# Later pairs' loads behind the first broadcast, and a fourth buffer for exponentials, in a planned attention and gated-MLP kernel

## Chip, cores and metric

The kernel runs on one core of one Trainium2 chip. The metric is device time in microseconds (us) of one execution; lower is better.

## What is computed

Eight batches, eight heads each, 576 positions, head dimension 64, all in float32. Per head, causal attention with a decay bias: the running sum `cum` of max(s, 0) along the sequence gives a bias -(cum_i - cum_j) for every query and key, cut at 0. The heads' outputs of one batch, side by side, are the 512 wide input of a gated MLP with a three-tap convolution along the sequence.

```python
def _attn_ref(q, k, v, s):
    scores = scale * np.matmul(q, k.transpose(0, 1, 3, 2))
    cum = np.cumsum(np.maximum(s, 0.0), axis=-1)
    bias = -(cum[:, :, :, None] - cum[:, :, None, :])
    scores = np.where(causal, -1000000000.0, scores + np.minimum(bias, 0.0))
    scores = scores - np.max(scores, axis=-1, keepdims=True)
    attn = np.exp(scores)
    attn = attn / (np.sum(attn, axis=-1, keepdims=True) + 1e-09)
    return np.matmul(attn, v)

def _moe_ref(x, w_in, conv_w, w_out):
    h = np.maximum(x @ w_in, 0.0)          # 512 -> 1024
    conv_out = ...                         # three taps along the sequence, per channel
    gate = 1.0 / (1.0 + np.exp(-conv_out))
    return (h * gate @ w_out)              # 1024 -> 512
```

## The kernel before

**Pairs.** Work is cut into 32 pairs of heads, four to a batch; `pair(p)` makes the tasks of one. A pair's queries and keys come in one load (`qk`, tile `raw`, line 1015). ACT or DVE rounds them to a high part (`hi`, line 1027), POOL or DVE takes the low rest (`lo`, line 1031), both in tile `s`. A shifted score is then formed to find each row's maximum: matmuls `sh` (line 1097), with a mask added by matmuls on line 1104 for the first seven pairs, and on DVE 12 reductions `mx` (line 1129) per pair that add the broadcast prefix sums `bb` (line 1059, a transfer that copies two rows of `cum_d` to all partitions) and keep the maximum in `r`. A transpose `turn` (line 1155), ACT `rt` (line 1163) and a DMA `ds` into `eq` (line 1171) bring the maxima into a row. Then come the 48 score matmuls `sc` (line 1208), 12 exponentials on ACT into `pt` (line 1223), five causal cuts `mk` on POOL (line 1241), the sums over keys `sum` (line 1323) and the product with the values `pv` (line 1266).

**The normalising chain.** After `sum`, ACT copies the sums (`gd`, guard, line 1339), a DMA regroups them (`rc`, line 1345), DVE takes the reciprocal (line 1350), a DMA writes it to DRAM (`ri`, line 1355), a DMA pair spreads it over the partitions (`rb`, line 1365), and DVE multiplies `pv` by it (`nm`, norm, line 1373); ACT and DVE or POOL then split the result into `x` (lines 1388, 1392). There is one set of buffers for `rs`, `rc` and `ri` together, taken by `gd` and given back when `rb` has landed, and one for `pv` in PSUM, given back by the norm.

**Gated MLP.** For each batch and half of the sequence, `h` (line 1423) are the matmuls with `w_in`, 12 to a block of 128 channels, and `o` (line 1512) those with `w_out`. `h` of a batch needs the four pairs of that batch and the weights, which are loaded (line 880), put together from 64 bit words and split into two parts on ACT, DVE and POOL during the first pairs.

**What sets the order.** Every piece of work is a task with a cost in us, the tasks that it needs and the buffers that it takes. `Sched.play` lets the five engines run through these costs, and each engine takes the ready task with the smallest due time; the due times are the table `DUE`, one number for a task, in sixteenths of a us. The order so found is what each engine runs, strictly in a row; a semaphore wait holds all that stands behind it. `opts` of a task names the engines that may do it and the cost on each; a third entry `True` keeps a DVE task and a POOL task that both have it from being planned at the same time. `follow(a, b)` offers `b` only when `a` has been started. Where PE would have nothing to do, the planner puts in a matmul on zeros (tile `still`, line 1559), up to its time 112.

**Buffers.** `BUFS` counts them. The fifth number, `NPT`, is that of `pt`, one for a head; a pair takes two at its first scores and gives them back after `sum` and `pv`. `setup` values share their room: `s_sb` and `ones` lie in `PT_t[1]`, `cum` and `grid` in `PT_t[2]`.

**The start.** `s` is loaded, DVE makes `cum` (lines 763, 764), then `grid` and `ncr` (lines 771 to 777); SP writes `cum` (line 789) and `ncr` (line 791) to DRAM and fetches the first broadcasts (line 1059). `bx` (lines 798, 802) are rows for the scores, stored to `rows_d` (line 815). POOL makes constants (`ident`, lines 716 to 731; `masks`, lines 702 to 709: a memset and four selects; `pads`, lines 737, 739). The first bias transposes on PE (line 830) take the PSUM bank of the first reduction.

Of the kernel before, what the change touches and what calls it, by code (L numbers as in the profile page):

```python
# [27 lines left out]
BUFS = 2, 2, 3, 3, 3, 5, 3, 2  # L28
# [520 lines left out]
def kernel(  # L549
# [192 lines left out]
    def c_ind(t):  # L742
        def run(e):
# [8 lines left out]
            c_pads(i))  # L752
        for i in range(NE)
    ]
    t_ident = add("ident", [("POOL", 4.3)], [], -189.5, c_ident)
    t_ind = [
        add(f"ind{i}", [("ACT", 0.72)], [t_masks], -187 + i, c_ind(EQ_t[i])) for i in range(NEQ)
    ]
# [216 lines left out]
    def link():  # L975
        for n, g in sorted(groups.items()):
# [6 lines left out]
            for (a, _), (c, _) in zip(seq, seq[1:]):  # L983
                sch.follow(a, c)

    direct = []
    last_ek, last_v, last_nm = [None], [None], []


    L = NT - 1  # L990
# [637 lines left out]
```

## Time and profile before

| | us |
|---|---|
| median of 3 runs | 767.01 |
| lowest and highest | 760.92, 767.8 |
| profiled execution | 766.71 |
| its span | 765.0 |
| granted TensorE clock, mean share | 0.989 |
| busy: PE, PEld, DVE, ACT, POOL | 744.2, 669.3, 513.5, 455.6, 363.1 |

The span runs from the first to the last instruction; the profiled execution was 1.7 us longer than its span. PE is the TensorE with its matmuls, PEld its weight loads, DVE VectorE, ACT ScalarE, POOL GpSimd, SP the engine that issues all DMAs here. A busy PE may be busy with matmuls on zeros, and at the lower of two clocks (2.4 and 1.2 GHz; 0.50 in a row is the lower one).

### The profile page before, as it was taken

Reading aid. Unit: us, or ns where it says so; the run is one execution under the profiler, and the core shown is the slowest. Engines: PE = TensorE matmul, PEld = TensorE weight load, DVE = VectorE, ACT = ScalarE, POOL = GpSimd, SP = SyncE. Lnnn points to the kernel's source line nnn. Section 1 sums busy time; section 2 is a strip of 40 time slices with the busy share of each in tenths; the row PEclk is TensorE's granted clock in tenths of the full one; section 3 lists DMA queues with packets and bytes.
Section 4 is the critical chain, followed back from the end, with each engine's and each line's share of the span. In section 5 each row is a group of like instructions: output and inputs, shape, how many; then the busy total and the mean of one; then the engine's idle time right before and its main releaser. Section 6 shows DMA issues by size and latency. Waiting matters only on the chain.

```text
span 765.0 us, 20449 instructions
## 1 busy us (share of the span) xinstructions
PE 744.2 (97%) x7868; PEld 669.3 (87%) x7868; DVE 513.5 (67%) x1404; ACT 455.6 (60%) x1070; POOL 363.1 (47%) x444
## 2 busy tenths in 40 slices
PE   8998999999999999999999999999999999999998
PEld 6675778898988888898988889898888999899998
DVE  7488987566776757677775776777686676633632
ACT  5276777375665656566674756556566646654643
POOL 6053435574566455545554655545435546612212
PEclk9599999999999999999999999999999999999999
DMA  6865852324333241424322342242414221111001
GB/s 192 262 212 185 271 185 66 129 66 128 93 106 111 56 128 65 128 93 122 98 79 87 98 132 79 78 143 80 127 48 122 90 82 43 43 41 40 17 25 39
DMA packets 55160, 80.18 MB, mean 105 GB/s; under 512 B 14042, under 2 KB 34842, under 8 KB 55002
## 3 DMA queue, kind: packets, MB, share of 16 engines
q1 hardware_dynamic: 55061, 78.87, 33.3%
q8 instruction: 61, 1.00, 0.5%
q14 instruction: 38, 0.30, 0.1%
HBM read 67.48 MB, written 10.98 MB: 103 GB/s over the span
## 4 chain that ended last, share of the span: by engine, by line
PE 79%; DVE 8%; issue 5%; DMA 4%; ACT 2%; POOL 1%; SPq 0%; DVEq 0%; POOLq 0%; ACTq 0%
PE ps L1423 25%; PE ps L1512 25%; PE ps L1208 11%; PE pv L1266 10%; PE ps L1097 4%; DVE ps L1129 3%; PE ps L1323 3%; DMA rb<-ri_d 2%; DMA ri_d<-ri 2%; ACT pt L1223 1%; PE ps L1559 1%; DVE r L1129 1%; DMA bb<-cum_d 1%; DVE ct L1454 1%; DVE rb L1373 1%
## 5 line engine op out<-in xcount | busy, mean ns | idle before, releaser
L1512 PE MATMUL ps<-u,wo 128*128 128x288 f32 x1536 | 218.2, 298 | 1.1 <-ACT ob L1529 0.5
L1423 PE MATMUL ps<-x,wi 128*128 128x290 f32 x1536 | 217.6, 298 | 0.3 <-DVE x L1392 0.2
L1423 PEld LDWEIGHTS ps<-x,wi 128*128 128x128 f32 x1536 | 209.2, 190 | 2.2 <-ACT pt L1223 0.5
L1512 PEld LDWEIGHTS ps<-u,wo 128*128 128x128 f32 x1536 | 206.9, 188 | 4.0 <-ACT pt L1223 1.7
L1223 ACT ACTIVATE pt<-ps,bias_sb 128x288 f32<-128x288 f32 (+4 forms) x384 | 152.9, 479 | 64.6 <-PE ps L1208 64.4
L1484 POOL TENSOR_TENSOR u<-ct,u 128x576 fp32r<-128x576 f32 x64 | 92.4, 1446 | 187.8 <-ACT u L1480 144.1
L1454 DVE SCALAR_TENSOR_TENSOR ct<-ps,cw_sb,ct 128x288 f32<-128x288 f32 (+1 forms) x256 | 130.2, 514 | 69.6 <-ACT ct L1441 67.1
L1129 DVE CUSTOM_DVE_ANT_0 ps<-ps,bb 128x64 f32<-128x64 f32 (+4 forms) x320 | 134.3, 451 | 47.3 <-PE ps L1097 23.1
L1208 PE MATMUL ps<-s 64*128 64x288 f32 (+4 forms) x1152 | 113.8, 304 | 8.6 <-DVE r L1129 7.5
L1208 PEld LDWEIGHTS ps<-s 64*128 64x128 f32 x1152 | 91.0, 187 | 17.3 <-DVE r L1129 12.4
L1241 POOL TENSOR_SCALAR_AFFINE_SELECT pt<-pt 128x256 f32<-128x256 f32 (+1 forms) x160 | 69.9, 450 | 74.6 <-ACT pt L1223 56.4
L1070 POOL TENSOR_SCALAR_AFFINE_SELECT bb<-bb 128x256 f32<-128x256 f32 (+1 forms) x125 | 52.6, 429 | 98.4 <-DVE r L1129 81.9
L1266 PE MATMUL pv<-pt,v 128*32 128x448 f32 (+4 forms) x1536 | 94.6, 389 | 3.3 <-DVE rb L1373 3.3
L1436 ACT ACTIVATE ps<-ps 128x289 f32<-128x289 f32 x128 | 50.8, 397 | 72.8 <-PE ps L1423 67.1
L1031 POOL TENSOR_TENSOR s<-raw,s 128x1152 fp32r<-128x1152 f32 x31 | 88.8, 2865 | 6.2 <-ACT s L1027 3.9
L1266 PEld LDWEIGHTS pv<-pt,v 128*32 128x32 f32 x1536 | 59.2, 110 | 34.6 <-issue 24.6
L1466 ACT ACTIVATE ct<-ct 128x288 f32<-128x288 f32 x128 | 56.2, 440 | 38.6 <-DVE ct L1454 38.0
L1472 DVE TENSOR_TENSOR ct<-ct,ps 128x288 f32<-128x288 f32 x128 | 57.1, 449 | 21.7 <-ACT ct L1466 20.9
L1441 ACT ACTIVATE ct<-ps,cw_sb 128x288 f32<-128x288 f32 x128 | 63.8, 500 | 5.0
L1097 PE MATMUL ps<-s 64*128 64x288 f32 (+4 forms) x384 | 60.3, 348 | 1.3 <-DVE ct L1472 1.1
L1208 PE MATMUL ps<-eq,ek 64*128 64x288 f32 (+4 forms) x384 | 59.7, 301 | 0.0
L1129 DVE DVE_READ_ACCUMULATOR2_ANT r<- 128x1 f32 x384 | 54.1, 141 | 0.0
(89 smaller groups left out, 700.6 us busy)
## 6 DMA issues: line engine op xcount, KB each, us to landing
raw<-qk SPq DMA_DIRECT2D x32, 576.0 KB
bb<-cum_d SPq DMA_DIRECT2D x32, 576.0 KB
v<-vp SPq DMA_DIRECT2D x32, 320.0 KB
rb<-ri_d SPq DMA_DIRECT2D x64, 144.0 KB
outT<-ob SPq DMA_DIRECT2D x64, 144.0 KB
w<-w_in SPq DMA_DIRECT2D x8, 512.0 KB
w<-w_out SPq DMA_DIRECT2D x8, 512.0 KB
rows_d<-bx SPq DMA_DIRECT2D x1, 1215.0 KB
```

The costliest lines, as they stand in the source:

```text
L1031: tt_on(e)(st[:, 0:2, :], R_t[raw.slot], st[:, 2:4, :].bitcast(F32), op=ALU.subtract)
L1097: nc.tensor.matmul(dst[j], l, S_t[sb.slot][r, 2, c0:c1], start=True, stop=not (early and diagonal(tau, c1)),)
L1129: nc.vector.tensor_tensor_reduce(out=src, in0=src, in1=in1, scale=1.0, scalar=acc if c0 else -3.0e38, op0=ALU.add, op1=ALU.max, accum_out=acc,
L1208: nc.tensor.matmul(dst[j], l, m, start=(k == 0), stop=(k == 3))
L1223: nc.scalar.activation(PT_t[pts[j].slot][0:jt, O_T[t] + c0 : O_T[t] + c1], bank(pb, o, o + c1 - c0)[0:jt], AF.Sigmoid, bias=bias_sb[0:jt, ...
L1241: nc.gpsimd.affine_select(out=reg, in_=reg, pattern=[[0, 2], [1, min(P, W_T[t])]], compare_op=ALU.is_ge, fill=0.0, base=0, channel_multipl ...
L1266: nc.tensor.matmul(pvt[gs, o0 : o0 + c1 - c0], vt[0:jt, t, gs], PT_t[pts[g // 2].slot][0:jt, O_T[t] + c0 : O_T[t] + c1], start=(t == 0), s ...
L1423: nc.tensor.matmul(bank(hb, 0, XW), l, r, start=(k == 0), stop=(k == len(seq) - 1))
L1441: nc.scalar.activation(C_t[ct.slot][:, i, :], bank(hb, 2 * hf, 2 * hf + HS), AF.Copy, scale=cw_sb[:, 3 * f + 1 : 3 * f + 2],)
L1454: nc.vector.scalar_tensor_tensor(cc[:, lo:hi], bank(hb, hf + sh + lo, hf + sh + hi), cw_sb[:, 3 * f + k : 3 * f + k + 1], cc[:, lo:hi], op ...
L1484: tt_on(e)(uu[:, 1], C_t[ct.slot], uu[:, 0].bitcast(F32), op=ALU.subtract)
L1512: nc.tensor.matmul(bank(pb, 0, HS), l, r, start=(fp == 0 and k == 0), stop=(fp == NF // 2 - 1 and k == len(seq) - 1),)
```

## The change

- `NPT`, the number of buffers for heads' exponentials, goes from 3 to 4 (one more 64x64 memset at the start).
- Loads of `raw` for pairs 2 and up are offered only after the first broadcast `bb0` has been started.
- In the planner, `bb0` counts 400,000 bytes more, and nine costs of setup tasks are changed; `cum`, `grid` (and `rest` as before) are kept apart in time from POOL tasks that have the same mark.
- The table `DUE` is a new one, of the same length. So the order is new on every engine.

```diff
-BUFS = 2, 2, 3, 3, 3, 5, 3, 2
+BUFS = 2, 2, 3, 3, 4, 5, 3, 2
...
-    -4437, -31564, -3194, -3762, -3297, -3396, -3426, -2970, -2895, -2949, -3684, -32749, -26067,
...
+    9452, 6483, 13492,
...
-    t_masks = add("masks", [("POOL", 3.6)], [], -190, c_masks)
+    t_masks = add("masks", [("POOL", 4.4)], [], -190, c_masks)
...
-    t_ident = add("ident", [("POOL", 4.3)], [], -189.5, c_ident)
+    t_ident = add("ident", [("POOL", 2.9)], [], -189.5, c_ident)
...
-    t_ones = add("ones", [("DVE", 0.4)], [], -298, lambda e: nc.vector.memset(ones, 1.0))
+    t_ones = add("ones", [("DVE", 0.55)], [], -298, lambda e: nc.vector.memset(ones, 1.0))
...
-    t_cum8 = add("cum", [("DVE", 2.0)], [t_s, t_ones], -170, cum_chain)
+    t_cum8 = add("cum", [("DVE", 2.0, True)], [t_s, t_ones], -170, cum_chain)
...
-    t_cum = add("grid", [("DVE", 2.4)], [t_cum8], -169, grid_chain)
+    t_cum = add("grid", [("DVE", 1.5, True)], [t_cum8], -169, grid_chain)
...
-    t_rest = add("rest", [("DVE", 1.6, True)], [t_cum], -140, rest)
+    t_rest = add("rest", [("DVE", 0.8, True)], [t_cum], -140, rest)
...
-    t_bmm = add("bias_mm", [("PE", 1.2)], [t_rest, t_ident], -140, bias_mm, alloc=[b_ps])
+    t_bmm = add("bias_mm", [("PE", 0.6)], [t_rest, t_ident], -140, bias_mm, alloc=[b_ps])
...
+    first_bb = []
...
         t_bb = add(f"bb{p}", [("SP", 0.4)], [t_cum_d], a_sh - BBA, load_bb, alloc=[bb],
-                   nbytes=2 * P * S * 4)
+                   nbytes=2 * P * S * 4 + (400_000 if p == 0 else 0))
+        if p == 0:
+            first_bb.append(t_bb)
+        elif p > 1:
+            sch.follow(first_bb[0], t_load)
```

All lines of the changed file lie 1 to 6 further down than in the one before.

The queue of SP at the start, before: `raw0`, `raw1` are the two buffers for queries and keys (pairs 2 and 3 use them anew), `bb0` and `bb1` those for the broadcasts.

```order
L789 DMA cum_d_111<-pt_96 64x576
L791 DMA base_d_112<-ncr_118 64x10
L1059 DMA bb0_91<-cum_d_111 128x2x576
L1015 DMA raw0_81<-qk 128x1152
L1059 DMA bb1_92<-cum_d_111 128x2x576
L787 DMA base_sb_93<-base_d_112 5x32x2 x2
```

The same rows of the change:

```order
L790 DMA cum_d_111<-pt_96 64x576
L792 DMA base_d_112<-ncr_118 64x10
L1061 DMA bb0_91<-cum_d_111 128x2x576
L1017 DMA raw0_81<-qk 128x1152
L1061 DMA bb1_92<-cum_d_111 128x2x576
L788 DMA base_sb_93<-base_d_112 5x32x2 x2
```

Nothing has moved here: the load of the third pair stood behind the first broadcast already.

DVE at the start, before, from the making of `ncr` to the first reduction (`s1` is pair 1, `s0` pair 0):

```order
L774 TENSOR_SCALAR ncr_118<-pt_96 64x9
L777 MEMSET ncr_118 64x1
L822 SCALAR_TENSOR_TENSOR pt_96<-pt_96 64x576
L802 TENSOR_SCALAR bx_119<-pt_96,ncr_118 64x576 x2
L895 SCALAR_TENSOR_TENSOR ct0_107<-ct0_107 128x24
L1031 TENSOR_TENSOR s1_84<-raw1_82,s1_84 128x1152
L1129 ISA ps4_69,r0_99<-ps4_69,bb0_91 128x64
```

DVE at the same place in the change:

```order
L775 TENSOR_SCALAR ncr_118<-pt_96 64x9
L778 MEMSET ncr_118 64x1
L1033 TENSOR_TENSOR s0_83<-raw0_81,s0_83 128x1152
L823 SCALAR_TENSOR_TENSOR pt_96<-pt_96 64x576
L803 TENSOR_SCALAR bx_119<-pt_96,ncr_118 64x576 x3
L1033 TENSOR_TENSOR s1_84<-raw1_82,s1_84 128x1152
L896 SCALAR_TENSOR_TENSOR ct0_107<-ct0_107 128x24
L902 SCALAR_TENSOR_TENSOR ct0_107<-ht_106,ct0_107 128x24
L1135 ISA ps0_65,r0_99<-ps0_65,bb0_91 128x288
```

The low parts of pair 0 have come to DVE, behind `ncr`; a third row set `bx` too; and the first reduction is now that on bank `ps0_65`, which the bias transposes wait for.

POOL at the start, before, after the last memset of `onehot`:

```order
L737 MEMSET ek2_87 128x640
L739 MEMSET ek2_87 10x576 x2
L1031 TENSOR_TENSOR s0_83<-raw0_81,s0_83 128x1152
L737 MEMSET ek1_86 128x640
L739 MEMSET ek1_86 10x576 x2
L702 MEMSET v1_95 128x640
L705 AFFINE_SELECT v1_95<-v1_95 64x640
```

POOL at the same place in the change:

```order
L703 MEMSET v1_95 128x640
L706 AFFINE_SELECT v1_95<-v1_95 64x640
L710 AFFINE_SELECT v1_95<-v1_95 64x640
L706 AFFINE_SELECT v1_95<-v1_95 64x640
L710 AFFINE_SELECT v1_95<-v1_95 64x640
L738 MEMSET ek1_86 128x640
```

The subtraction for pair 0 has left POOL, and the memset and four selects of `masks` have come to the front.

ACT after the exponentials of pair 0, before; L891 and L886 are weights, L1339 is the guard of pair 0, and the exponentials on L1223 behind it are those of pair 1:

```order
L1223 ACTIVATE pt_96<-ps0_65,bias_sb_76 128x320
L891 ACTIVATE w1_5122_356<-w1_10240_354,tail_sb_78 128x512
L886 ACTIVATE w1_5121_355<-w1_10240_354 128x512
L886 ACTIVATE w0_5121_352<-w0_10240_351 128x512
L891 ACTIVATE w0_5122_353<-w0_10240_351,tail_sb_78 128x512
L886 ACTIVATE w2_5121_358<-w2_10240_357 128x512
L891 ACTIVATE w2_5122_359<-w2_10240_357,tail_sb_78 128x512
L1339 ACTIVATE rs_103<-ps1_66 128x144
L938 CAST wi_79<-w1_5122_356 128x4x128
L938 CAST wi_79<-w0_5122_353 128x4x128
L1163 ACTIVATE rt0_101<-ps0_65,base_sb_93 10x64 x2
L1223 ACTIVATE pt_96<-ps1_66,bias_sb_76 128x288
```

ACT at the same place in the change:

```order
L1229 ACTIVATE pt_96<-ps1_66,bias_sb_76 128x320
L887 ACTIVATE w1_5121_361<-w1_10240_360 128x512
L892 ACTIVATE w1_5122_362<-w1_10240_360,tail_sb_78 128x512
L887 ACTIVATE w2_5121_364<-w2_10240_363 128x512
L892 ACTIVATE w2_5122_365<-w2_10240_363,tail_sb_78 128x512
L1229 ACTIVATE pt_96<-ps1_66,bias_sb_76 128x288
L1229 ACTIVATE pt_96<-ps3_68,bias_sb_76 128x288
L1229 ACTIVATE pt_96<-ps4_69,bias_sb_76 128x288
L1229 ACTIVATE pt_96<-ps5_70,bias_sb_76 128x288
L887 ACTIVATE w0_5121_358<-w0_10240_357 128x512
L892 ACTIVATE w0_5122_359<-w0_10240_357,tail_sb_78 128x512
L1345 ACTIVATE rs_103<-ps0_65 128x144
```

With the fourth buffer, four exponentials of pair 1 stand ahead of the guard of pair 0. On PE likewise: 16 of pair 1's 48 score matmuls stand before the sums of pair 0 and the other 32 before its `pv`, where before all 48 stood behind `pv`.

## Rows read from the trace of the kernel before

**Rows 1.** The page: the span, and the granted TensorE clock in 40 equal slices of it, in tenths of full speed.

```profile
span 765.0 us, 20449 instructions
...
PEclk9599999999999999999999999999999999999999
```

**Rows 2.** Busy time of each engine in four stretches (from:to, length, then PE, PEld, DVE, ACT, POOL busy with their instructions, granted clock, DMA share, GB/s).

```profile
0.00:17.60 17.60, 14.76 (x119) 11.55 (x119) 13.11 (x27) 9.95 (x14) 13.27 (x29) 1.00 0.56 174
17.60:34.70 17.10, 17.09 (x88) 10.78 (x90) 9.59 (x46) 2.52 (x8) 0.00 (x0) 0.50 0.95 296
34.70:105.50 70.80, 67.24 (x965) 49.52 (x963) 58.40 (x170) 52.86 (x117) 29.67 (x36) 1.00 0.66 213
105.50:740.00 634.50, 623.23 (x6543) 575.82 (x6540) 423.97 (x1147) 379.37 (x908) 315.85 (x376) 1.00 0.29 89
```

**Rows 3.** The matmuls on zeros (line 1559) in the stretch from 34.7 to 105.5 us, as a group of PE's lines (busy us, mean ns of one), and the group of `pv` there with the idle time before it and who ended it.

```profile
L1559 PE MATMUL ps<-still 64*128 64x256 bf16 (+1 forms) x104 | 14.8, 272 | 0.1
L1266 PE MATMUL pv<-pt,v 128*32 128x448 f32 (+4 forms) x240 | 14.6, 390 | 3.3 <-DVE rb L1373 3.3
```

**Rows 4.** Timeline of the start (start us, length us, engine, line, operation; in brackets the idle time before it and who ended it): DVE, POOL and SP.

```profile
7.07 3.22 DVE L774 TENSOR_SCALAR ncr<-pt 64x9 f32<-64x9 f32 x1
9.65 0.74 DVE L822 SCALAR_TENSOR_TENSOR pt<-pt 64x576 f32<-64x576 f32 x1
10.33 1.71 DVE L802 TENSOR_SCALAR bx<-pt,ncr 64x576 fp32r<-64x576 f32 x2
12.06 1.34 DVE L1031 TENSOR_TENSOR s<-raw,s 128x1152 fp32r<-128x1152 f32 x1
...
3.44 0.63 POOL L737 MEMSET ek<- 128x640 f32 x1
7.06 2.64 POOL L1031 TENSOR_TENSOR s<-raw,s 128x1152 fp32r<-128x1152 f32 x1 [1.55 <-ACT s L1027]
12.69 1.29 POOL L705 TENSOR_SCALAR_AFFINE_SELECT v<-v 64x640 f32<-64x640 f32 x1
14.05 0.71 POOL L709 TENSOR_SCALAR_AFFINE_SELECT v<-v 64x640 f32<-64x640 f32 x1
...
5.79 0.50 SPq L789 DMA_DIRECT2D cum_d<-pt  x1
10.35 0.46 SPq L791 DMA_DIRECT2D base_d<-ncr  x1
```

**Rows 5.** The chain of waits, in order of time (start us, us, what).

```profile
10.86 5.21 DMA bb<-cum_d
...
48.22 3.72 DMA ri_d<-ri
...
52.57 5.11 DMA rb<-ri_d
...
57.77 0.76 DVE rb L1373
...
77.30 3.53 PE ps L1208 x48
...
101.83 0.77 DVE rb L1373
```

**Rows 6.** Stretches of 1 us with the same columns as Rows 2.

```profile
8.00:9.00 1.00, 1.00 (x9) 0.52 (x10) 1.00 (x1) 1.00 (x2) 1.00 (x1) 1.00 0.00 0
...
16.00:17.00 1.00, 0.00 (x0) 0.00 (x0) 0.75 (x5) 0.65 (x2) 0.32 (x1) 1.00 1.01 410
...
18.00:19.00 1.00, 0.99 (x5) 0.49 (x3) 1.00 (x7) 0.33 (x1) 0.00 (x0) 0.50 1.68 438
```

**Rows 7.** Timeline of DVE and PE from the first reduction to the first scores.

```profile
9.59 6.28 PE L1559 MATMUL pv<-still 64*128 64x256 bf16 x56
16.25 0.23 DVE L1129 CUSTOM_DVE_ANT_0 ps<-ps,bb 128x64 f32<-128x64 f32 x1 [2.85 <-DMA bb<-cum_d]
17.59 0.70 PE L830 MATMUL ps<-ident,pt 64*128 64x64 f32 x5 [1.71 <-DVE r L1129]
26.91 4.23 PE L1559 MATMUL ps<-still 64*128 64x256 bf16 x19
28.23 0.40 DVE L1129 CUSTOM_DVE_ANT_0 ps<-ps,bb 128x192 f32<-128x192 f32 x1
32.55 1.09 PE L1208 MATMUL ps<-s 64*128 64x288 f32 x6
```

**Rows 8.** Timeline of pair 0 after its scores: exponentials, weights and guard on ACT, sums on PE, and the first matmuls of the MLP.

```profile
33.91 1.85 ACT L1223 ACTIVATE pt<-ps,bias_sb 128x288 f32<-128x288 f32 x4 [1.82 <-PE ps L1208]
36.11 2.99 ACT L1223 ACTIVATE pt<-ps,bias_sb 64x64 f32<-64x64 f32 x8 [0.35 <-PE ps L1208]
39.63 1.24 ACT L886 ACTIVATE w<-w 128x512 f32<-128x512 f32 x2
41.73 1.77 PE L1323 MATMUL ps<-pt,onehot 128*32 128x144 f32 x54
43.60 0.29 ACT L1339 ACTIVATE rs<-ps 128x144 f32<-128x144 f32 x1 [0.82 <-PE ps L1323]
...
105.48 1.88 PE L1423 MATMUL ps<-x,wi 128*128 128x290 f32 x12
```

**Rows 9.** The group of the `sh` matmuls over the whole span (busy us, mean ns of one).

```profile
L1097 PE MATMUL ps<-s 64*128 64x288 f32 (+4 forms) x384 | 60.3, 348 | 1.3 <-DVE ct L1472 1.1
```

468 rows, old and new, of the table DUE are left out of this document.

## Prediction

> **What bounds the kernel now.** I read the page first, then busy time by stretches, then the chain of waits and the timeline of the first 110 us. The span is 765.0 us, and the profiled execution took 766.71 us, 1.7 us more, close to the median of 767.01 us, so the sum is made against 766.7 [rows 1]. From 105.5 to 740 us PE is busy for 623.23 of 634.50 us at full clock and runs no matmul on zeros: PE bounds this stretch, and its work there is the same in the change [rows 2]. What can be won lies before 105.5 us. There PE seems busy too, but much of it is not work. In the first 17.6 us hardly any work is done. From 17.6 to 34.7 us the granted clock is 0.50, the lower of the two levels [rows 2]. From 34.7 to 105.5 us PE spends 14.8 us on 104 matmuls on zeros and waits 3.3 us, all of it for the norm, while DVE is busy 58.4 of 70.8 us and ACT 52.9 [rows 2, 3].
>
> In that last stretch the normalising chain sets the pace. The norm of pair 0 starts at 57.77 us and that of pair 3 at 101.83: three rounds in 44.06 us, 14.7 us each [rows 5]. Within the first, the reciprocals' store takes 3.72 us and the spread 5.11 [rows 5]. There is one set of buffers for this, so a guard can come only after the last spread has landed, and `pv` of the next pair waits for the norm. The first matmul of the MLP is at 105.48, 3.65 us after the start of norm 3 [rows 5, 8].
>
> **The change, part by part.**
>
> *The loads behind the first broadcast.* In the queue of SP the third pair's load already follows `bb0`, and the rows there are the same in both orders. So the new rule by itself moves nothing and is costed at 0, between -0.5 and +0.5 us for later loads, nearest to the equal rows.
>
> *DVE's start.* The making of `ncr` takes 3.22 us, beside a subtraction on POOL of 2.64 us; the broadcasts' write `base_d` waits for it until 10.35, and `bb0` stands behind that and goes at 10.86 [rows 4, 5]. In the change the subtraction is on DVE, behind `ncr`. A tensor-scalar of ten columns is at most as long as one of `bx`, 0.86 us, so `ncr` ends at 7.2 to 7.9 instead of 10.30, and `base_d` can go 2.4 to 3.1 us sooner. Then `bb0` waits for `cum_d`, issued at 5.79: the DMA engines are idle from 8 to 9 us [rows 4, 6], so I put its landing at 8.5 and the issue of `bb0` there, 2.3 us sooner; with its 5.21 us it lands at 13.7 instead of 16.07 [rows 5]. DVE by then has done, from 7.2 on, two subtractions of 1.34, 0.74, three `bx` of 0.86 and two small ones of about 0.2, some 6.4 us, and is free at 13.6 [rows 4]. The first reduction starts at 13.8, not 16.25 [rows 7].
>
> *PE's wait and the clock.* PE ends its 56 zeros at 15.87, stands still until 17.59 because the bias transposes need a bank that the third reduction gives free, and in the slice from 18 us the clock is 0.50 [rows 6, 7]. In the change the 57 zeros (0.112 us each, after 45 instead of 48 at the start) end at about 15.6, and the bank's reduction is now the first, done at 14.4. The wait of 1.71 us is gone, and I expect the clock to stay at its upper level.
>
> *From the first reduction to the first scores.* 24 reductions of the two pairs take from 16.25 to 28.63 before, 12.4 us with the waits among them [rows 7]. In the change they take 13.8 to 26, less some 1.5 us of waits for a slow PE and plus 1 us for the bias. The second transpose then stands ready at 26, after 19 zeros that took 4.23 us at half clock and take half of that at full. Seven zeros and the scores follow: 27.5 us instead of 32.55 [rows 7]. At half clock this would be 30.
>
> *Pair 0 to its guard.* Before, the exponentials start 1.36 us after the scores and take until 39.1, and the guard starts at 43.60 [rows 7, 8]. In the change ACT begins at 28.9 and needs 4.9 us for 12 exponentials; then four weight passes of 0.62 (2.5 us), four exponentials of pair 1 (1.85), two more passes (1.3): 39.5 [rows 8]. Beside this, POOL's cuts and PE's sums are done by 38. I take the guard at 39.8, with 0.3 for handing over: 3.8 us sooner. The scores came 5 us sooner; the pieces that now stand ahead of the guard take 1.2 us back.
>
> *The rounds.* The chain's buffers are not changed. Four rounds of 14.7 us lead from guard 0 to norm 3, now at 98.0. Per round the same transfers lie between (a broadcast, values, keys, two or three weights), in other places, and SP now has a load of `ek` that waits for the next pair's scores ahead of the store. I take no change, with 0.8 us a round to either side.
>
> *The fourth buffer.* With it, scores may run ahead of `pv`. By the first MLP matmul the order has 296 score matmuls instead of 240, 92 `sh` instead of 84, one more transpose, and as many sums and `pv`. At 3.53 us for 48 and 0.157 for one `sh` this is 4.1 + 1.3 + 0.3 = 5.7 us of work done by then that before came later [rows 5, 9]. The MLP's first matmul stands behind eight of these score and six `sh` matmuls, 0.6 + 0.9 = 1.5 us, so it comes 3.65 + 1.5 after norm 3, at 103.2 instead of 105.5. The gain is 2.3 + 5.7 = 8.0 us. PE has room for that: 27 zeros fewer behind the first scores are worth 3.8 us [rows 3], and the rest comes from the 5 us at the start. The extra memset and PE's allocations lie beside other work.
>
> *The rest.* Behind 105.5 us idle time is 11.3 us of 634.5 [rows 2]. A new table may move this by 3 us either way; I take 0.
>
> Sum: 766.7 - 8.0 = 758.7, say 758.8 us.
>
> **A rule of the skill against it.** In the trace, a select of `masks` takes 1.29 us when it starts beside DVE's subtraction and 0.71 alone, and `ncr` stood still beside POOL's subtraction [rows 4]. In the change the four selects run from about 4.1 us beside the prefix sums. If each can hold up one of DVE's steps for its 0.71 us, `ncr` ends at 10.0, `bb0` goes at 10.5, and all that follows is 2 us later, while PE's wait is still gone or short: 760.8. The Trainium skill, SBUF — State Buffer, section Who interferes with whom, says that VectorE and GpSimd share a pair of ports under an exclusive lock, that whichever starts first holds it for its whole instruction, and that the other "fully blocks"; the trace agrees with its 3.22 us, and by that rule the planner's mark on `cum` and `grid` doesn't protect them, as `masks` has none.
>
> **Rivals.**
> - *The lock:* as above, 760.8. For it: the two rows. Against: memsets on POOL beside the same DVE steps, from 3.44 us on, delayed nothing [rows 4].
> - *The clock falls all the same:* the reductions still pace PE with short waits from 17 to 26 us. Scores at 30 instead of 27.5, guard at 42: 766.7 - 8.0 + 2.5, plus a first score block at half speed, about 762.
> - *The rounds grow by 1.5 us:* the chain is longer by what now stands ahead on ACT and SP. 4 x 1.5 = 6 us back: 765. The same time comes out if the change does not do what it says and only the order is another.
> - *Slower:* the load of `ek` ahead of the reciprocals' store waits for scores which wait for banks that ACT frees only behind the guard. Each round is held by 4 us: 16 - 8 = 8 us, 775. It turns slower than now from 2 us a round.
> - *More:* rounds shorter by 0.8 us and less idle time in the MLP stretch: 754.
>
> **How the numbers follow.** The measurement tells about 1% from no change, 7.7 us, so faster means below 759.3. Chances: the forecast 0.48 (755.5 to 762, six in ten of it below 759.3), more 0.12, the lock 0.12, the clock 0.12, grown rounds 0.10, slower 0.06. Faster: 0.29 + 0.12 + 0.02 + 0.02 = 0.45; slower 0.06; the same 0.49. The range goes from 752 to 768: it leaves out the slower case and a tail of the better one.
>
> **What would show it.** In the changed profile: `ncr` short and `bb0` issued near 8.5 us; no PE wait at 16 us and a clock of 1.00 from 16 to 35; the first scores near 27.5, the guard of pair 0 near 39.8, norms 14.7 us apart, norm 3 near 98, the first MLP matmul near 103; from there the same idle time. Selects of 1.3 us or a late `ncr` would show the lock; waits of SP ahead of the reciprocals' store the grown rounds. Wrong most easily: the length of a round, which counts four times.

## The result, and the profile after

| | before | after |
|---|---|---|
| median of 13 executions, us | 766.40 | 770.76 |
| lowest and highest | 760.57, 769.38 | 767.59, 775.25 |
| profiled execution, its span | 766.71, 765.0 | 773.5, 771.8 |
| mean granted clock of that execution | 0.989 | 0.991 |

The ratio is 1.0079, 95% interval 1.0054 to 1.0103: the change costs 0.8%. I had forecast 758.8 us, a gain of 1%, and a range that ended at 768.

The page of after: span, and granted clock in 40 slices.

```profile
span 771.8 us, 20376 instructions
...
PEclk9989999999999999999999999999999999999999
```

Half of the plan worked: the 5 in [rows 1] is gone. But an 8 stands in the third slice, where before had a 9.

Stretches of after, cut at its own first MLP matmul, 113.24 us (columns as in [rows 2]; the last three rows are stretches of 1 us).

```profile
17.60:34.70 17.10, 16.85 (x163) 12.61 (x163) 11.42 (x54) 5.77 (x17) 3.35 (x4) 1.00 0.92 285
34.70:113.24 78.54, 68.34 (x942) 49.19 (x938) 59.20 (x173) 55.16 (x121) 35.42 (x43) 0.91 0.65 201
113.24:771.80 658.56, 644.35 (x6637) 594.04 (x6637) 414.74 (x1144) 386.54 (x917) 323.06 (x380) 1.00 0.28 85
47.00:48.00 1.00, 0.25 (x4) 0.12 (x2) 0.08 (x1) 0.89 (x2) 0.79 (x3) 1.00 1.00 361
...
49.00:50.00 1.00, 0.00 (x0) 0.00 (x0) 0.97 (x2) 0.95 (x2) 0.00 (x0) 0.50 0.86 250
93.00:94.00 1.00, 1.00 (x7) 0.68 (x5) 0.68 (x2) 1.00 (x4) 1.00 (x1) 0.50 0.73 279
```

The same last stretch of before, from its first MLP matmul to the end:

```profile
105.48:765.00 659.52, 645.08 (x6708) 597.43 (x6702) 432.37 (x1165) 390.32 (x933) 320.15 (x379) 1.00 0.28 86
```

Three things are to be seen. From 17.6 to 34.7 us the clock is at its upper level, as forecast ([rows 2]: 0.50). From 34.7 us to the first MLP matmul the mean clock is 0.91, which makes some 14 of 78.5 us at the lower level (an estimate from the mean), and that stretch is 78.5 us instead of 70.8. From the first MLP matmul on, after needs 658.56 us for 65 weight loads fewer (6,637 for 6,702), where before needs 659.52: the work that was brought forward is missing there, but the time isn't.

What PE waited for from 26 to 114 us in after (us in total, times, longest):

```profile
PE ps L1329 <- DVE r L1135: 4.4, 1, 4.4
PE ps L1103 <- ACT pt L1229: 2.5, 1, 2.5
PE ps L1565 <- ACT rt L1169: 1.9, 1, 1.9
PE ps L1214 <- ACT rs L1345: 1.1, 1, 1.1
```

Before, the only waits of PE there were 3.3 us for the norm [rows 3]. After, 0.2 us is for the norm, and the rest for reductions, exponentials, a bias copy and a guard. The largest is read from the chain of waits of after (start us, us, what):

```profile
45.21 5.10 DMA bb<-cum_d
...
50.44 0.63 DVE ps L1135
...
51.60 3.34 PE ps L1329 x41
54.94 0.56 PE ps L1103 x2
...
57.28 0.62 DVE rb L1379
...
57.94 2.18 PE pv L1272 x25
```

In before the chain to norm 0 runs through the reciprocals' store and the spread [rows 5]. Here it runs through a broadcast of prefix sums, `bb3`, that pair 3's reductions need. It lands at 50.31. The sums of pair 1 stand on PE behind one of these reductions, because they use its bank, so PE stands still; products stand behind the sums, two reductions behind those products, and norm 0 behind those in DVE's row.

Why `bb3` is so late is seen in the timeline of after. SP:

```profile
40.50 1.24 SPq L1351 DMA_DIRECT2D rc<-rs  x2
...
42.71 0.94 SPq L881 DMA_DIRECT2D w<-w_in  x2
44.30 0.34 SPq L1361 DMA_DIRECT2D ri_d<-ri  x1
45.21 0.37 SPq L1061 DMA_DIRECT2D bb<-cum_d  x1
```

PE, and DVE below it:

```profile
41.64 0.33 PE L1103 MATMUL ps<-s 64*128 64x320 f32 x2
...
51.60 3.34 PE L1329 MATMUL ps<-pt,onehot 128*32 128x144 f32 x56 [4.35 <-DVE r L1135]
```

```profile
43.20 0.35 DVE L1135 CUSTOM_DVE_ANT_0 ps<-ps,bb 128x192 f32<-128x192 f32 x1
...
50.44 0.63 DVE L1135 CUSTOM_DVE_ANT_0 ps<-ps,bb 128x448 f32<-128x448 f32 x1 [0.38 <-DMA bb<-cum_d]
```

There are two buffers for broadcasts, so `bb3` needs pair 2's to be used up. Pair 2's last products (41.64) now stand on PE behind the sums of pair 0 and scores of pair 1. That scores of pair 1 stand so early only a fourth buffer for exponentials allows; that the products stand behind them is the new table's choice. And five weight passes of DVE, from 40.32 on, stand ahead of pair 2's four last reductions (43.20 to 45.19); the products were done by then, so the passes end last. Only then can SP send `bb3`.

### The profile page after: what moved, and what is told of

It reads as the page before. It is cut to its first block, busy times and chain, and to the rows that moved or that the text cites. A ratio compares the mean times of both kernels' runs of the same rounds, so it can differ in the third digit from the quotient of the medians.

```text
span 771.8 us, 20376 instructions
## 1 busy us (share of the span) xinstructions
PE 745.4 (97%) x7852; PEld 668.1 (87%) x7852; DVE 500.0 (65%) x1397; ACT 457.6 (59%) x1068; POOL 373.4 (48%) x454
## 4 chain that ended last, share of the span: by engine, by line
PE 81%; DVE 6%; DMA 5%; issue 3%; ACT 3%; POOL 0%; SPq 0%; DVEq 0%; POOLq 0%; ACTq 0%
PE ps L1518 25%; PE ps L1429 24%; PE ps L1214 12%; PE pv L1272 11%; PE ps L1103 4%; PE ps L1329 4%; DMA w<-w_in 2%; DVE ps L1135 2%; DMA bb<-cum_d 2%; DVE ct L1460 1%; ACT pt L1229 1%; DMA ek<-bx 1%; DMA ek<-rows_d 1%; DVE r L1135 1%; PE ps L1161 0%
## 5 line engine op out<-in xcount | busy, mean ns | idle before, releaser
L1429 PE MATMUL ps<-x,wi 128*128 128x290 f32 x1536 | 220.1, 299 | 2.8 <-DVE ct L1478 2.3
L1460 DVE SCALAR_TENSOR_TENSOR ct<-ps,cw_sb,ct 128x287 f32<-128x287 f32 (+1 forms) x256 | 130.0, 514 | 80.2 <-ACT ct L1447 75.1
L1135 DVE CUSTOM_DVE_ANT_0 ps<-ps,bb 128x192 f32<-128x192 f32 (+4 forms) x320 | 133.8, 452 | 58.0 <-PE ps L1103 30.7
L1214 PE MATMUL ps<-s 64*128 64x288 f32 (+4 forms) x1152 | 118.1, 304 | 8.0 <-DVE r L1135 5.8
L1214 PEld LDWEIGHTS ps<-s 64*128 64x128 f32 x1152 | 94.9, 185 | 18.0 <-DVE r L1135 12.2
L1272 PE MATMUL pv<-pt,v 128*32 128x448 f32 (+4 forms) x1536 | 96.4, 395 | 0.2 <-DVE rb L1379 0.2
L1033 POOL TENSOR_TENSOR s<-raw,s 128x1152 fp32r<-128x1152 f32 x30 | 85.0, 2832 | 8.3 <-ACT s L1029 8.3
L1272 PEld LDWEIGHTS pv<-pt,v 128*32 128x32 f32 x1536 | 58.2, 111 | 34.2 <-issue 27.0
L1214 PE MATMUL ps<-eq,ek 64*128 64x288 f32 (+4 forms) x384 | 63.7, 299 | 0.0
L1103 PE MATMUL ps<-s 64*128 64x288 f32 (+4 forms) x384 | 59.2, 345 | 2.6 <-ACT pt L1229 2.5
```

The source lines that it names most:

```text
L1033: tt_on(e)(st[:, 0:2, :], R_t[raw.slot], st[:, 2:4, :].bitcast(F32), op=ALU.subtract)
L1103: nc.tensor.matmul(dst[j], l, S_t[sb.slot][r, 2, c0:c1], start=True, stop=not (early and diagonal(tau, c1)),)
L1135: nc.vector.tensor_tensor_reduce(out=src, in0=src, in1=in1, scale=1.0, scalar=acc if c0 else -3.0e38, op0=ALU.add, op1=ALU.max, accum_out=acc,
L1214: nc.tensor.matmul(dst[j], l, m, start=(k == 0), stop=(k == 3))
L1272: nc.tensor.matmul(pvt[gs, o0 : o0 + c1 - c0], vt[0:jt, t, gs], PT_t[pts[g // 2].slot][0:jt, O_T[t] + c0 : O_T[t] + c1], start=(t == 0), s ...
L1429: nc.tensor.matmul(bank(hb, 0, XW), l, r, start=(k == 0), stop=(k == len(seq) - 1))
```

## The experiments

In all edits `put(names, ahead)` moves tasks in the order found by the planner to directly ahead of another task; `zeros(n, ahead)` adds matmuls on zeros. The clock differs from one execution of the same program to the next, so each median mixes several; where it matters, executions of like clock are compared.

**The load rule.** After, with the third pair's load ahead of `bb0` again:

```diff
+    put("qk2", "bb0")
```

> The changed kernel, with one thing undone: the load of the third pair's queries and keys stands in SP's queue ahead of the first broadcast of prefix sums again, nothing else moves. If the order of these two transfers matters, the first broadcast, issued at 9.13 us in the changed kernel, comes some 0.4 us later and shares the engines with 576 KB more, so it lands 1 to 2 us later, pair 0's reductions follow, and the end is 1 to 1.5 us later: 772. Rival: the second broadcast (issued 10.28, 8.04 us to land) and PE's own work end this stage, so nothing moves: 770.8.

Measured: 772.95 us (767.26 to 778.13), ratio to before 1.0107 (1.0065 to 1.0150); after had 1.0079. `bb0` goes 1.1 us later (10.26), but first scores and first sums come at the same times as in after (28.0, 36.0). The median is higher by executions at a clock of 0.982 and less, which after has none of; at 0.996 and 0.997 three take 767.26 to 770.95 us, and after at 0.996 to 0.998 767.59 to 769.40. The rule that gives the change its name has no effect that can be seen here.

**The start alone.** Before, with only the start of the change, three buffers, and before's order for the rest:

```diff
+    by["lo0"].eng = "DVE"
+    put("ones", "still")
+    put("tail", "pads0")
+    put("lo0", "rest")
+    put("masks", "pads2")
```

> The kernel before (three buffers, its own order) with the new start alone: the subtraction for pair 0's low halves on DVE in place of POOL, DVE's and POOL's start in the order of the change; from the first scores on every engine keeps the order of before. Theory of the prediction: PE no longer waits 1.71 us at 15.9, the clock stays at 1.00 in 17.6 to 34.7, pair 0's guard comes 3 to 4 us earlier and the rounds take 14.7 us as before: 758 to 761. Rival: the next wait (pair 3's broadcast, weights) takes the gain back whatever the order is: 765 to 767.

Measured: 764.16 us (760.89 to 766.28), 0.9984 (0.9956 to 1.0013), between the two expected ranges. PE's wait of 1.71 us [rows 7] is gone, and the clock falls all the same, in stretches of 1 us:

```profile
17.00:18.00 1.00, 0.82 (x5) 0.42 (x5) 1.00 (x6) 0.00 (x0) 0.00 (x0) 1.00 1.02 284
18.00:19.00 1.00, 1.00 (x7) 0.57 (x8) 0.28 (x2) 0.00 (x0) 0.00 (x0) 0.72 1.23 329
19.00:20.00 1.00, 0.89 (x5) 0.37 (x3) 0.57 (x3) 0.00 (x0) 0.00 (x0) 0.50 0.85 203
```

PE is busy for 0.82 to 1.00 of each of these, and the longest wait behind the first zeros is 0.18 us. That it is enough to end the wait of 1.71 us, as I had it, is refuted.

**Zeros for the clock, three times.** In before (e6), in before with the new start (e7), and in after (e2, in front of the three waits):

```diff
# e6, before
+    zeros(14, "bias_mm")
+    zeros(6, "sh1.0")
+    zeros(4, "sh1.1")
# e7, before with the new start
+    zeros(4, "bias_mm")
+    zeros(6, "sh1.0")
+    zeros(4, "sh1.1")
# e2, after
+    zeros(36, "sum1")
+    zeros(20, "nm1")
+    zeros(14, "rt5")
```

> The kernel before, with 24 more zero matmuls on PE between 15.9 and 20 us: 14 ahead of the transposes that wait until 17.59 and 10 ahead of the next products. Nothing else moves. Theory: the kernel before has a clock drop of 17.07 us in this place in its profile, and its executions fall into two groups by the clock of the whole run: 759.7 to 762.0 where it is 1.000, some 767 where it is 0.989. If the empty stretch brings the drop, the zeros hold the clock and nearly all executions are at 760 to 762. Rival: the drop has another cause, and the median stays at 766 or loses up to 1 us to the zeros.

> The new start alone on the kernel before (as in the run start alone, 764.16), with 14 more zero matmuls on PE behind pair 0's first products. Theory of the clock: the start alone still fell to half clock at 18.45 us in its profile though PE no longer waited 1.7 us; its executions at a clock of 1.000 took 760.9 to 762.6. With PE filled as it is in the changed kernel (x22 matmuls in 16 to 18 us against x15) the clock stays at 1.00 and the median is 760 to 762. Theory of the prediction (an earlier start is worth its 3 to 4 us where the order behind it is that of before): 757 to 759. Rival: the drop stays: 764.

> The changed kernel, with 36, 20 and 14 more zero matmuls on PE, at the places of its idle stretches at 47.2, 71.2 and 91.0 us: the waits stay, only the clock is kept. Theory of the clock: no drop at 48.5 and 92.9; the 3.8 and 6.8 us that PE worked at half clock shrink by half, 5.3 us, and the time is 765.5. Theory of the waits: what follows each gap waits for DVE and ACT and not for PE, so a full clock gives back 2 us at most: 769. If the zeros stand in the way, 771 to 773.

Measured: e6 764.82 us, 0.9999 (0.9969 to 1.0029): the mean clock is at least 0.995 in every execution (in 31 of before's 102), so zeros in this place mostly keep it, but in a late start they cost what the clock gives. e7 **762.24 us (759.69 to 764.38), 0.9956 (0.9931 to 0.9982)**: the fastest kernel of this study. Its first scores come at 27.6 us, its first MLP matmul at 101.1, and seven of twelve executions keep a clock of 1.000. These take 759.69 to 762.60 us, and before at 1.000 takes 759.65 to 762.96: what e7 wins over before is the clock, and the earlier start of the prediction (757 to 759 expected) isn't to be seen in the time. But e7 has the change's start, with first scores as late as in after (27.6 and 27.9), ahead of three buffers and before's order, and is at its first MLP matmul 12.2 us sooner than after. So nearly all of the loss, with the falls of the clock at 48 and 93 us, arises behind the start. No run has four buffers with before's table, or three with the new one, so these two parts of the change are not told apart.

e2 771.94 us, 1.0081 (1.0053 to 1.0108). Its stretches, cut at its own first MLP matmul:

```profile
34.70:110.20 75.50, 71.33 (x1008) 53.46 (x1007) 58.95 (x170) 55.36 (x121) 35.31 (x43) 1.00 0.67 210
110.20:769.10 658.90, 644.28 (x6639) 593.89 (x6637) 415.57 (x1144) 386.93 (x918) 322.78 (x379) 1.00 0.28 85
```

The clock is 1.00 throughout, and the first MLP matmul comes 3.0 us sooner than in after; the median isn't better, as expected for zeros that stand in the way. What the falls cost by themselves e2 can't say: after's own executions take 767.59 to 769.40 us at 0.996 to 0.998 (three) and 772.92 to 775.25 at 0.988 and 0.989 (three), some 5 us apart. What made the waits remains: before at 0.996 to 0.998 takes 762.02 to 763.74 (eight), again some 5 us less.

**The price of the work that was brought forward.** 65 matmuls of pairs 5 to 7 taken out of both kernels: in after they lie ahead of the first MLP matmul, in before behind it.

```diff
+    for n in "sc5.0 sc5.1 sc5.2 sc5.3 sc6.0 tn6 sh7.0 sh7.1 sh7.2".split():
+        by[n].emit = lambda e: None
```

> The kernel before, leaving out on PE the 65 matmuls that the changed kernel runs ahead of its first expert matmul and the kernel before behind it: the scores of pair 5, the first scores of pair 6, a transpose, three products of pair 7. All that reads them stays. Theory of the prediction (PE is the bound behind the first expert matmul, so work brought forward comes back in full): 5.7 us less, 760.5. Rival (the stage waits for other engines in these places, and what is taken off PE becomes waiting): 0 to 2 us less, 764 to 766.

> The changed kernel, leaving out on PE the same 65 matmuls as the run on the kernel before (scores of pair 5, first scores of pair 6, a transpose, three products of pair 7), which it runs ahead of its first expert matmul. Theory (work brought forward is paid in full up front, and hardly comes back): first expert matmul at 107 to 108.5 us in place of 113.2, from there to the end 658 to 659 as with them, 765 us. Rival (PE waits there for other engines anyway, the work is free): first expert matmul at 111 or later and 769 to 771.

Measured: e8 762.98 us, 0.9980 (0.9945 to 1.0015). Its six executions at a clock of 0.997 to 1.000 take 759.4 to 761.8 us (median 760.8); before's 27 there take 759.65 to 763.74 (761.2). e9 769.58 us, 1.0047 (1.0018 to 1.0075); its first MLP matmul is at 110.7 us, 2.5 sooner than in after, not 5.7, near the rival's values. In before the 65 matmuls cost little or nothing; in the profiled execution waits take their place. The stretch of e8 from its first MLP matmul, and PE's new wait in it:

```profile
99.90:759.20 659.30, 641.81 (x6645) 594.33 (x6637) 430.70 (x1165) 390.68 (x933) 320.18 (x379) 1.00 0.29 86
```

```profile
106.28 0.94 PE L1423 MATMUL ps<-x,wi 128*128 128x290 f32 x5 [2.18 <-ACT pt L1223]
```

PE is busy 3.3 us less than in before and idle 3.1 us more; the stretch is as long. After has the same 6,637 weight loads there and needs 658.56. So my 5.7 us were not to be had: the stretch takes 657 to 660 us in the profiled execution of every kernel here, with those matmuls or without.

e8 has a second use: its profiled execution keeps the clock up, so it shows before's first stage without the fall:

```profile
37.76 1.24 SPq L1345 DMA_DIRECT2D rc<-rs  x2
39.09 0.41 SPq L1059 DMA_DIRECT2D bb<-cum_d  x1
```

```profile
7.08 0.16 DVE L774 TENSOR_SCALAR ncr<-pt 64x9 f32<-64x9 f32 x1
...
51.43 0.76 DVE L1373 TENSOR_TENSOR rb<-pv,rb 128x576 f32<-128x576 f32 x1 [1.09 <-DMA rb<-ri_d]
```

First scores are at 25.7 us, the guard's store at 37.76, `bb3` at 39.09, norm 0 at 51.43, the first MLP matmul at 99.91. After has 27.9, 40.50, 45.21, 57.13 and 113.24. Against such an execution of before, the change is 2.2 us behind at the scores, 2.7 at the guard, 6.1 at `bb3`, 5.7 at norm 0, 11.1 at norm 3 (96.27 and 107.41) and 13.3 at the first MLP matmul.

**Pieces of the convolution's weights later.** After, to free the first reduction from a wait of 1.04 us for ACT:

```diff
+    put("cw1 cw2 cwh", "mx0.0.0.0")
```

> The changed kernel, with the small passes over the convolution's weights moved on DVE from ahead of pair 0's first reduction to behind its seventh. In the changed kernel DVE waited 1.04 us for ACT there, and the first reduction came at 15.33 where the prediction had 13.8. Theory (this wait is a part of the late start): first reduction at 14.0 to 14.3, first scores 0.5 to 1 us earlier than 27.9; in the time at most 1 us, 769.8 to 770.8. Rival: the second broadcast lands at 18.3 whatever DVE does, and neither scores nor time move.

Measured: 771.53 us (769.27 to 774.29), 1.0060 (1.0035 to 1.0085). The first reduction moves from 15.33 to 14.95 only, as it then waits for `bb0` to land; the scores come 0.9 us sooner, but the guard of pair 0 (40.03) and `bb3` (45.07) hardly, and the first MLP matmul is at 113.7. That us at the scores is lost before the guard.

**`bb3` and what stands around it, in three steps.** After, with guard 0 and the last reductions of pair 2 ahead of weight passes (e4); in addition pair 3's reductions ahead of weight passes (e10); in addition pair 2's last product ahead of pair 1's scores, and `bb3` and the reciprocals ahead of weight loads (e14). Five further moves, the same in all three and not shown, are for the later waits.

```diff
# e4
+    put("gd0", "wo0q")
+    put("mx2.1.1.0 mx2.1.2.0 mx2.0.1.0 mx2.0.2.0", "wi3l")
+    put("bb3", "wi0")
...
# e10: e4 and
+    put("mx3.0.3.0 mx3.0.0.0 mx3.1.4.0 mx3.1.0.0 mx3.1.4.288 mx3.0.4.0 mx3.1.3.0 mx3.0.4.288", "wi0q")
+    put("wo0h wi2l wo0l", "wi0q")
# e14: e10 with these in place of e4's second and third
+    put("sh2.3", "sc1.2")
+    put("mx2.1.1.0 mx2.1.2.0 mx2.0.1.0 mx2.0.2.0", "wo01")
+    put("bb3", "dr4")
+    put("inv0", "wi3l")
+    put("ri0", "wi0")
+    put("rb0", "wi1")
```

> The changed kernel, with the order changed at four places of the stage before the first expert matmul, always in one way: an ACT or DVE pass over expert weights (or its load) no longer stands ahead of a step of a pair that was ready. Guard of pair 0 ahead of a piece of the output weights; pair 2's last four reductions ahead of three weight passes; the broadcast for pair 3 ahead of two weight loads in SP's queue; the passes over three later pieces behind the exponentials, turned sums and guards that stood behind them. Theory of the weights: the gaps of 1.1, 4.4, 2.5 and 1.9 us on PE shrink to under 1 us each, the clock stays at 1.00, the first expert matmul comes at 104 to 107 us in place of 113.2, and the time is 761 to 764. Theory of the clock alone: the gaps stay in part, the drops go: 765.5. Theory that the loss is behind the first expert matmul: not below 767.

> As the run with later weights, and in addition the first eight reductions of pair 3 stand on DVE ahead of four passes over weights and of the three that wait for the next load. In that run the empty stretch at 47 us had grown from 4.4 to 7.3, since the passes that waited for a load issued 1.2 us later still stood ahead of these reductions. Theory of the weights: the stretch shrinks to 1 to 2 us, no drop of the clock, first expert matmul at 105 to 108 us, 765 to 767. Rival (the pairs' chain has another wait behind it): first expert matmul at 110 or later, 769 to 771.

> The changed kernel, with pair 2's last two products put back on PE ahead of pair 1's last scores, their four reductions ahead of the pass over a piece of the output weights on DVE, and, on SP, the broadcast for pair 3 behind them ahead of two loads of keys, the store of pair 0's reciprocals ahead of two weight loads, the spread of the reciprocals ahead of a third; besides the moves of the run with pair 3 early. Theory: the chain of pairs was late by its broadcast (issued 45.21 us in the changed kernel; 39.09 in the run on the kernel before at full clock, where these products stand ahead of pair 0's sum), so here it is issued at 41 to 42 us, the empty stretch at 47 us is gone, norm 0 comes at 51.5 to 54 in place of 57.1, the first expert matmul at 107 to 109, and the time is 763.5 to 766. Rival (the chain is held by the store and load of the reciprocals and by weights, whatever the broadcast does): norm 0 at 56 or later and 768 to 770.

Measured: e4 771.11 us, 1.0073 (1.0045 to 1.0101). It missed: PE's wait at 47 us grew from 4.35 to 7.3 us, since pair 3's reductions now stood behind a DVE weight pass at 51.16 that waited 2.79 us for ACT, which had itself waited 4.71 us for a load of `w_in`. Moving one task ahead of the weights only moves the wait to the next. e10 768.34 us, 1.0048 (1.0024 to 1.0071): `bb3` at 43.54, PE's wait 2.8 us, but the spread `rb` goes at 51.37, behind weight loads. The expected 761 to 764 and 765 to 767 us were both missed. e14 **766.50 us (764.87 to 769.20), 1.0010 (0.9983 to 1.0036)**: 4.3 us better than after, 0.5 above its expected range. SP of e14, its norm 0, and PE's largest waits from 26 to 115 us:

```profile
42.20 0.39 SPq L1061 DMA_DIRECT2D bb<-cum_d  x1
...
47.10 1.22 SPq L1371 DMA_DIRECT2D rb<-ri_d  x2
```

```profile
56.07 0.75 DVE L1379 TENSOR_TENSOR rb<-pv,rb 128x576 f32<-128x576 f32 x1
```

```profile
PE pv L1272 <- DVE rb L1379: 2.6, 2, 2.2
PE ps L1329 <- DVE r L1135: 1.2, 1, 1.2
```

`bb3` goes 3.0 us sooner, PE's wait for the reductions is 1.2 us instead of 4.35, and the first MLP matmul comes at 109.1 instead of 113.24. So what stands at the heads of the queues is shown to be a cause: the moves together take back 4.3 of the 9.8 us between after's median and before's at full clock (760.96). A part of that is the clock: at 0.996 to 0.998 the median of e14's eleven executions is 766.4, that of after's three 767.67.

The broadcast alone is not this cause. In e4 and e10 `bb3` went 1.7 us sooner too, and norm 0 came at 59.29 and 57.14, no sooner than in after (57.13). In e14 it comes at 56.07 where I had expected 51.5 to 54, and so has the rival's sign, though not its time: the spread was issued at 47.10, but on DVE seven weight passes (51.00 to 55.28) and two reductions now stand ahead of the norm.

## Why the prediction was wrong, point by point

*The load rule, 0 us.* Right (e1).

*DVE's start.* The direction was right, the sizes not. `ncr` is made from 8.01 to 8.58 us instead of by 7.2 to 7.9, and `bb0` goes at 9.13, not 8.5:

```profile
4.51 1.75 DVE L765 TENSOR_TENSOR_SCAN pt<-pt 64x576 f32<-64x576 f32 x1
...
8.01 0.57 DVE L775 TENSOR_SCALAR ncr<-pt 64x9 f32<-64x9 f32 x1
...
15.33 0.47 DVE L1135 CUSTOM_DVE_ANT_0 ps<-ps,bb 128x288 f32<-128x288 f32 x1
```

The rival of the lock acted in part: beside the selects the prefix sum takes 1.75 us, where before it took 1.35. And the 3.22 us of [rows 4] that I removed are not there in every execution: e8, with the start of before, makes `ncr` in 0.16 us, and its first reduction starts at 13.40, ahead of after's 15.33. I took one execution's delay as fixed.

*PE's wait and the clock.* The result was right (no wait, 1.00 from 0 to 48 us), the reason was not (e5).

*Scores and guard.* 27.89 for 27.5, and 40.16 for 39.8: right in the number, in part by luck. The first reduction is 1.5 us late (15.33 for 13.8), and what lies between it and the scores takes 12.6 us where I had 13.7.

*The rounds: the step that failed.* From guard 0 to norm 3 I put 58.2 us, as before (four times 14.7, as I wrote, would be 58.8). The norms of after, first as one line's instructions (duration, first and last start), then norms 1 and 2, and norms 1 and 2 of before in its chain:

```profile
L1379 DVE TENSOR_TENSOR rb<-pv,rb x4: 753/757/758, 57.1 to 107.4; 128x576 f32<-128x576 f32 x4
```

```profile
72.85 0.76 DVE L1379 TENSOR_TENSOR rb<-pv,rb 128x576 f32<-128x576 f32 x1 [1.94 <-DMA rb<-ri_d]
...
93.32 0.76 DVE L1379 TENSOR_TENSOR rb<-pv,rb 128x576 f32<-128x576 f32 x1 [0.53 <-DMA rb<-ri_d]
```

```profile
73.32 0.77 DVE rb L1373
...
87.14 0.67 DVE rb L1373
```

From 40.16 to 107.4 it is 67.2, 9.0 us more: 2.8 up to norm 0, where the guard's lead of 3.4 us was lost, and 6.2 in the three rounds. They are not all longer: they take 15.7, 20.5 and 14.1 us, in before 15.6, 13.8 and 14.7 [rows 5]. The loss is the second round, from norm 1 to norm 2. All runs with after's table have it (19.0 to 23.1 us, e14 19.0); e7, with before's order, takes 13.9. In it the guard of pair 2 starts 3.7 us behind norm 1, in before 0.25 ahead of it (73.07). ACT and PE of after there:

```profile
70.13 0.77 ACT L892 ACTIVATE w<-w,tail_sb 128x512 uint32<-128x512 uint8 x1 [1.77 <-DMA w<-w_out]
...
76.58 0.29 ACT L1345 ACTIVATE rs<-ps 128x144 f32<-128x144 f32 x1 [1.18 <-PE ps L1329]
```

```profile
73.65 0.42 PE L1103 MATMUL ps<-s 64*128 64x320 f32 x2 [2.49 <-ACT pt L1229]
```

The guard waits for the sums of pair 2, which end at 76.55 us; in before they end at 71.75, ahead of norm 1. Two things stand before them on PE. One is the wait: weight passes that wait for loads of `w_out` stand on ACT ahead of an exponential, and two products wait for that. The other is the work brought forward: 32 of pair 3's 48 score matmuls, some 2.4 us, which in before come behind the `pv` that follows norm 1. Most of the rest of the round's growth lies in the spread: 6.9 us from its issue to the norm, 4.8 in before. In e14 the wait is gone, but the sums still end 3.1 us behind norm 1, with the same scores ahead of them, and the guard stands behind four weight passes besides; so the wait by itself isn't what makes this round long.

I had read the chain of store and spread as the length of a round, a property of the buffers. It was that in before's order, where PE had 14.8 us of zeros in that stretch [rows 3]. In after the chain from norm 1 to the first MLP matmul runs through a weight load and PE's own rows:

```profile
82.49 7.75 DMA w<-w_in
...
95.81 4.79 PE pv L1272 x48
```

ACT waits 5.2 us for loads of `w_in` from 26 to 114 us, and 1.8 in before's like stretch:

```profile
ACT w L887 <- DMA w<-w_in: 5.2, 4, 2.3
```

```profile
ACT w L886 <- DMA w<-w_in: 1.8, 2, 1.2
```

A pass that waits at ACT's head holds exponentials and bias copies behind it; PE's wait of 1.9 us for `rt`, and the clock's second fall at 93 us, follow such a one. The rival of grown rounds came nearest, at 1.5 us a round and a chance of 0.10; the slower rival's border of 2 us a round is about the measured mean, but its mechanism isn't there: the stores of the reciprocals go at 44.30 and 82.05, within 0.3 us of the reciprocals, so no load of `ek` holds them.

*From norm 3 to the first MLP matmul.* 5.8 us for 5.15: 0.7 late. With 0.4 at the guard and 9.0 from there to norm 3 this gives 113.24 for 103.2.

*The fourth buffer's 5.7 us: the second step that failed.* From the first MLP matmul on I expected 653.8 us and measured 658.56, 1.0 less than before. I had taken PE, busy for 98% of that stretch, as its bound, and so any work taken off it as time. e8 shows that this work has next to no price of its own there. After has a new wait of PE for DVE,

```profile
PE ps L1429 <- DVE ct L1478: 2.3, 4, 0.9
```

but others are shorter, and its idle time there is as in before (14.2 and 14.4 us). What is missing in after is busy time: 644.35 us, where e8 with as many weight loads has 641.81. Why the same work keeps PE busy for longer is not shown.

Together the 10.0 us up to the first MLP matmul and these 4.7 make the miss of 14.7 us between 758.8 and the profiled 773.5.

*The base.* At a clock of 1.000 before takes 759.65 to 762.96 us (20 executions); at 0.989 and less 765.6 to 772.4 (50). My gain was counted from an execution with the fall. All that the fall can give back is the 6.5 us between the medians of the two, and no execution of after with a clock from 0.994 up is under 767.59, where before's 31 take 759.65 to 765.41.

*What stays open.* Up to the first MLP matmul after is 13.3 us behind before at full clock (113.24 and 99.91). e14 takes back 4.1 of these, part of it by the clock. Of the other 9.2, 4.6 lie ahead of norm 0 (56.07 and 51.43), 1.2 between norms 0 and 3, where a short third round hides a second that is still 4.6 us longer, and 3.3 behind norm 3. No run puts the sums of pair 2 back ahead of pair 3's scores, so that their place is a cause of the long second round is read from the traces only. How much of the loss the fourth buffer has and how much the new table, and why the last stretch takes 657 to 660 us with the work or without, was not tried.

## What to carry to other kernels

The period of a chain measured in one order is not a constant of its buffers: before work is put into its slack, ask which task will then stand at the head of each queue (here passes over weights on ACT and DVE), and look at each round by itself, since a mean hides the one that failed. Work brought forward into a stage repays later only if the later stage is bound by its amount; take it out and measure before counting on it. And look at several executions: a delay or a low clock in the profiled one may be absent in many of them.

## What was not expected of the hardware

- The clock falls in some executions of a program and not in others: of 102 executions of before with a clock on record, 20 had a mean of 1.000 and 50 of 0.989 or less, and the medians of the two groups are 6.5 us apart (760.96 and 767.47).
- PE need not stand still for it: in e5 the clock fell between 18 and 19 us with PE busy for 0.82 to 1.00 of each us around it, while in after a wait of 2.5 us at 71 us brought no fall and one of 1.9 us at 91 us did.
- Which of DVE's steps stands still beside POOL's subtraction hangs on a tenth of a us. In before the subtraction starts at 7.06 us, 0.01 ahead of `ncr`, and `ncr` takes 3.22. In e8 it starts at 7.18, 0.10 behind `ncr`, which takes 0.16; a row set of `bx` further on takes 3.45 instead of 0.86. By the Trainium skill (SBUF — State Buffer, Who interferes with whom) whichever starts first holds the port; both traces agree.
